# Attention probabilities scaled before they are transposed, values as the stationary operand

## The chip, the cores and the metric

One core of a Trainium2 chip runs the whole program. The engines are TensorE (PE; the loads of its stationary operand are a row of their own, PEld), VectorE (DVE), ScalarE (ACT), GpSimd (POOL) and SyncE (SP), which issues nearly all DMAs. The metric is the device time of one execution in microseconds (us), less is better.

## The reference

Local attention (4 batches, 8 heads, 512 local and 32 global positions, head size 64), then a gated feed-forward block with an RMS norm, then a second feed-forward block with a rational activation.

```python
s_g = scale * q_g @ [k_g, k_l].T;  out_g = sm(s_g) @ [v_g, v_l]
s_ll = where(|i - j| <= 32, scale * q_l @ k_l.T, -1e9)
s_l = [scale * q_l @ k_g.T, s_ll]; out_l = sm(s_l) @ [v_g, v_l]
sm(s) = e / (sum(e) + 1e-9),  e = exp(s - max(s))
x = concat(out_g, out_l) as (4*544 rows, 512 features)
xn = x / rms(x) * rms_g
x = (silu(xn @ w_gate) * (xn @ w_val)) @ w_out
h = x @ w_in;  g = P(h) / (Q(h) + 1e-6);  out = g @ w_out2
```

## The kernel before

**Local attention.** The work is cut into 32 pieces s: a batch, a pair of heads (hp) and a half (u) of the 512 queries. For a piece, 256 queries of two heads are taken in windows of 32 queries, and each window sees 96 local keys and the 32 global ones, so that the scores of a piece are four blocks of 128 queries by 128 keys. Block i = 2c + hf is column half c of head hf; within a block the four windows j stand on partition groups of 32. A piece goes through four stages. `scores(s)` (L353 to L382): 32 short matmuls into two PSUM banks psS, four masked maxima on DVE (L377), four exponentials on ACT (L382) into the tile p. `trans(s)` (L384): four 128x128 transposes on PE into psT (L387), and one ACT copy to pt. `pv(s)` (L391): 16 matmuls into psO (L397), each with a 32-query slice of pt as the stationary operand and 65 columns of vw as the moving one: 64 features and a column of ones, which makes the sum of the row's exponentials. The four windows j use four column strips of the array. DVE then adds 1e-9 (L407), takes the reciprocal (L408) and scales the psO block into on (L410). `out(s)` (L412): two transposes on PE into psX (L416), since the next block wants features on partitions, and an ACT copy into x (L420).

**Global attention** has 8 quads qd of four heads: `g_scores` (psG, L428 and L432; exponentials with their sums at L440 and L441), `g_trans` (five transposes in two banks psGT, L452), `g_pv` (20 matmuls into psOg, L459, and the scaling on DVE, L471), `g_out` (a transpose into psGX, L478, and two DVE copies into x, L482).

**Both share PSUM.** Eight banks are in three rotations: "big" has four (psS, psG and the gate and value products psg, psv of the first feed-forward block), "t" has two (psK, psQ, psKG, psT, psGT, psX, psGX), "o" has two (psO, psOg, and of the feed-forward block psA and psN). A new tile of a rotation waits until the tile two (or four) before it has been read out.

**Order.** The outer loop runs t from 0 to LAST = 32 + TAIL - 1. `step(t)` (L492) makes the transposed keys and queries of piece t (psK, psQ, both from L325), takes piece t-1 through `trans`, t through `scores`, t-2 through `pv` and t-3 through `out`, with the quads of global attention at fixed steps. Between the parts it calls units of the first feed-forward block (60 of its 288 units are issued within the attention; they start at t = 5). A scheduler then orders each engine's instructions; attention has the higher priority (offset 50), the norms (L586 on, three stages for each block of rows, psN at L593) one higher still. The norm of a block is set up at t % 4 == 2. Weights are fetched, split and converted in steps on ACT, DVE and POOL (L83 to L109) from the start on. DMAs of the attention are issued by SP in a fixed order (`dma`, L212 to L219): the load of the values of piece s+4 stands in `pv(s)`, as it overwrites the values that `pv(s)` reads, and everything that SP issues later is behind it.

Of the kernel before, what the change touches and what calls it, by code (L numbers as in the profile page):

```python
# [128 lines left out]
class Attention:  # L129
# [3 lines left out]

    NP = B * H // 2
    NS = 2 * NP
    TAIL = 4
    VW = 65

    def __init__(self, tc, pool, x, stage, q_l, k_l, v_l, q_g, k_g, v_g, more):
        self.tc, self.nc, self.pool, self.x = tc, tc.nc, pool, x  # L140
# [61 lines left out]
        for vw in self.vw[2:]:  # L202
            nc.gpsimd.memset(vw, 1.0)
        nc.gpsimd.memset(self.pg[:, 544:], 0.0)
        self.kts, self.qts, self.pt, self.ptt, self.on, self.gq, self.stage = {}, {}, {}, {}, {}, {}, {}
        for i in range(2):
            self.spread_v(i)
            self.load_v(2 + i)
# [53 lines left out]
            self.dma(out=self.gin[32 * i : 32 * i + 32], in_=g[b].rearrange("h j d -> j h d"))  # L262

    def load_v(self, s):

        b, hp, u = self.place(s)
        t = self.vw[s % 4]  # L270
        v = self.v_l[b, 2 * hp]
        dma = self.dma

        def cut(h0, h1, w0, w1):
            dma(
                out=t[32:64, h0:h1, w0:w1, 0:D],
                in_=bass.AP(
                    tensor=v.tensor,
                    offset=v.offset + (h0 * SL + 32 * (8 * u + w0 - 1)) * D,
                    ap=[[D, 32], [SL * D, h1 - h0], [32 * D, w1 - w0], [1, D]],  # L280
                ),
            )

        for hf in range(2):
            cut(hf, hf + 1, (b, hp, u, hf) == (0, 0, 0, 0), 9 if (b, hp, u, hf) == (B - 1, 3, 1, 1) else 10)
        if u == 1:
            for hf in range(2):
                vg = self.v_g[b, 2 * hp + hf]
                dma(
                    out=t[96:128, hf, 1:9, 0:D],  # L290
                    in_=bass.AP(tensor=vg.tensor, offset=vg.offset, ap=[[D, 32], [0, 8], [1, D]]),
                )
# [60 lines left out]
    def scores(self, s):  # L353
        nc = self.nc
        b, hp, u = self.place(s)
        kt, qt, kg = self.kts[4 * b + hp], self.qts.pop(s), self.kgt[b % 2]
        ps = [self.bank(0, f"psS{s}_{hf}") for hf in range(2)]
        for c in range(2):
            for j in range(4):
                w = 8 * u + 4 * c + j  # L360
                for k0, keys in ((0, kt[:, 32 * w : 32 * w + 96]), (96, kg[:, hp, :])):
                    for hf in range(2):
                        rows = slice(64 * hf, 64 * hf + 64)
                        nc.tensor.matmul(  # L364
                            ps[hf][32 * j : 32 * j + 32, 128 * c + k0 : 128 * c + (96 if k0 == 0 else 128)],
                            qt[rows, 128 * c + 32 * j : 128 * c + 32 * j + 32],
                            keys[rows],
                            start=True, stop=True,
                        )
        p = self.work.tile([128, 4, 128], F32, tag="p", name=f"p{s}", bufs=self.wb[0])  # L370
        self.pt[s] = p
        nm = self.nm[:, s % 4]
        for c in range(2):
            m = self.masks[2 if (u, c) == (1, 1) else (0 if (u, c) == (0, 0) else 1)]
            for hf in range(2):
                i = 2 * c + hf
                self.last_ttr = nc.vector.tensor_tensor_reduce(  # L377
                    out=p[:, i], in0=ps[hf][:, 128 * c : 128 * c + 128], in1=m, scale=-SCALE, scalar=3.0e38,
                    op0=ALU.add, op1=ALU.min, accum_out=nm[:, i : i + 1],
                )  # L380
        for i in range(4):
            self.last_exp = nc.scalar.activation(out=p[:, i], in_=p[:, i], func=AF.Exp, scale=-1.0, bias=nm[:, i : i + 1])  # L382

    def trans(self, s):  # L384
        nc, p, ps = self.nc, self.pt.pop(s), self.bank(1, f"psT{s}")
# [3 lines left out]
        nc.scalar.activation(out=o, in_=ps, func=AF.Copy)  # L389

    def pv(self, s):  # L391
        nc, o, ps, v = self.nc, self.ptt.pop(s), self.bank(2, f"psO{s}"), self.vw[s % 4]
        for c in range(2):
            for hf in range(2):
                i = 2 * c + hf
                for j in range(4):
                    nc.tensor.matmul(  # L397
                        ps[32 * j : 32 * j + 32, self.VW * i : self.VW * i + D + 1],
                        o[:, 128 * i + 32 * j : 128 * i + 32 * j + 32],
                        v[:, hf, 4 * c + j + 1, 0 : D + 1],  # L400
                        start=True, stop=True,
                    )
        if s + 4 < self.NS:
            self.load_v(s + 4)
        ps = ps[:, 0 : 4 * self.VW].rearrange("q (i d) -> q i d", i=4)
        dn = self.dn[:, s % 4]
        nc.vector.tensor_scalar_add(dn, ps[:, :, D], 1e-9)  # L407
        nc.vector.reciprocal(out=dn, in_=dn)  # L408
        self.on[s] = on = self.work.tile([128, 4, D], F32, tag="on", name=f"on{s}", bufs=2)
        nc.vector.tensor_tensor(out=on, in0=ps[:, :, 0:D], in1=_ap(dn, [[1, 4], [0, D]]), op=ALU.mult)  # L410

    def out(self, s):  # L412
        nc, on, ps = self.nc, self.on.pop(s), self.bank(1, f"psX{s}")
        b, hp, u = self.place(s)
        for c in range(2):
            nc.tensor.transpose(  # L416
                ps[:, 128 * c : 128 * c + 128], on[:, 2 * c : 2 * c + 2, :].rearrange("q h d -> q (h d)"), self.ident
            )
        xo = self.x[b][hp // 2][:, hp % 2, SG + 256 * u : SG + 256 * u + 256]
        nc.scalar.activation(out=xo, in_=ps[:, 0:256], func=AF.Copy)  # L420

    def g_scores(self, qd):
# [16 lines left out]
        gs = self.gs[:, qd % 2]  # L439
        nc.scalar.activation(out=P[:, 0:512], in_=ps[0], func=AF.Exp, scale=SCALE, bias=gm[:, 0:1], accum_out=gs[:, 0:1])  # L440
        nc.scalar.activation(out=P[:, 512:544], in_=ps[1][:, 0:SG], func=AF.Exp, scale=SCALE, bias=gm[:, 0:1], accum_out=gs[:, 1:2])  # L441

    def g_trans(self, qd, part):
        nc, P = self.nc, self.pg
# [9 lines left out]

    def g_pv(self, qd):
        nc, o, ps = self.nc, self.gq.pop(qd), self.bank(2, f"psOg{qd}")
        for n in range(5):
            for g in range(4):
                nc.tensor.matmul(  # L459
                    ps[32 * g : 32 * g + 32, 0:D],  # L460
                    o[:, n, 32 * g : 32 * g + 32],
                    self.vn[(2 * qd + g // 2) % 3][:, g % 2, n],
                    start=(n == 0),
                    stop=(n == 4),
                )
        gs = self.gs[:, qd % 2]
        nc.vector.tensor_scalar(out=gs[:, 0:1], in0=gs[:, 0:1], scalar1=gs[:, 1:2], scalar2=1e-9, op0=ALU.add, op1=ALU.add)
        nc.vector.reciprocal(out=gs[:, 0:1], in_=gs[:, 0:1])
        og = self.pool.tile([128, 2, D], F32, tag="og", name=f"og{qd}", bufs=1)
        self.gq[qd] = og  # L470
        nc.vector.tensor_scalar(  # L471
            out=og, in0=_ap(ps, [[0, 2], [1, D]]), scalar1=gs[:, 0:1], scalar2=None, op0=ALU.mult
        )

    def g_out(self, qd):
        b, hq = divmod(qd, 2)
        ps = self.bank(1, f"psGX{qd}")
        self.nc.tensor.transpose(ps[:, 0:128], self.gq.pop(qd).rearrange("q h d -> q (h d)"), self.ident)  # L478
        for hf in range(2):
            rows = slice(64 * hf, 64 * hf + 64)  # L480
            src = ps[rows, 0:128].rearrange("d (p h i) -> d p h i", p=2, h=2)[:, :, hf, :]
            self.nc.vector.tensor_copy(self.x[b][hq][rows, :, 0:SG], src)  # L482

    def advance(self, s, to):

        if not 0 <= s < self.NS:
            return
        while self.stage.get(s, 0) < to:
            now = self.stage[s] = self.stage.get(s, 0) + 1
            (self.scores, self.trans, self.pv, self.out)[now - 1](s)  # L490

    def step(self, t, between):  # L492

# [12 lines left out]
        elif t in (0, 1):  # L506
            self.spread_v(t + 2)
        if t in (4, 8):
            for to in (2, 3, 4):
                for s in range(t - 4, t):  # L510
                    self.advance(s, to)
                    between()
# [6 lines left out]
            self.load_vn(4 * b + i - 3)  # L519
        between()  # L520
        self.advance(t - 2, 3)
        self.advance(t - 3, 4)
        for q0, first in ((0, 4), (1, 5)):
            n = i - first
            if t < NS:
                qd = 2 * b + q0
                if n == 0:
                    self.g_scores(qd)
                if n == 1:
                    between()  # L530
                    self.g_trans(qd, 0)
                    self.g_trans(qd, 1)
                if n == 2:
                    self.g_pv(qd)
                    if q0 == 0:
                        self.load_vn(2 * qd + 3)
                    between()
                    self.g_out(qd)


class FFN1:
# [247 lines left out]
def kernel(  # L789
# [7 lines left out]
    nc = tc.nc  # L797
# [76 lines left out]
    for t in range(LAST + 1):  # L874
# [8 lines left out]
            unit()  # L883
        if t == 2:
            load_consts()
        if t % 4 == 2 and t > 12:
            norms.append(ffn.norm(ORD[(t - 6) // 4]))
        elif t in (4, 8):
            norms.append(ffn.norm(ORD[t // 4 - 1]))
        with tc.high_priority(offset=200):  # L890
# [107 lines left out]
```

## Time and profile before

| | us |
|---|---|
| median of 3 runs | 1048.06 (1048.04 to 1048.88) |
| the profiled execution | 1043.17 |
| its span, first to last instruction | 1041.4 |
| PE busy in the span | 987.8 (95%) |
| DVE busy | 779.1 (75%) |
| ACT busy | 633.0 (61%) |
| POOL busy | 189.2 (18%) |

The mean granted clock of TensorE is 0.977 of full speed. In the page's chain that ended last PE has 80%, DVE 9%, DMA 5%, ACT 3% and SP 1%. Attention lasts from the start to about 300 us. The rest of the span is the two feed-forward blocks, whose instructions the change does not touch.

### The profile page before, as it was taken

Reading aid. Unit: us, or ns where it says so; the run is one execution under the profiler, and the core shown is the slowest. Engines: PE = TensorE matmul, PEld = TensorE weight load, DVE = VectorE, ACT = ScalarE, POOL = GpSimd, SP = SyncE. Lnnn points to the kernel's source line nnn. Section 1 sums busy time; section 2 is a strip of 40 time slices with the busy share of each in tenths; the row PEclk is TensorE's granted clock in tenths of the full one; section 3 lists DMA queues with packets and bytes.
Section 4 is the critical chain, followed back from the end, with each engine's and each line's share of the span. In section 5 each row is a group of like instructions: output and inputs, shape, how many; then the busy total and the mean of one; then the engine's idle time right before and its main releaser. Section 6 shows DMA issues by size and latency. Waiting matters only on the chain.

```text
span 1041.4 us, 23568 instructions
## 1 busy us (share of the span) xinstructions
PE 987.8 (95%) x9376; PEld 900.6 (86%) x9376; DVE 779.1 (75%) x1848; ACT 633.0 (61%) x1442; POOL 189.2 (18%) x220
## 2 busy tenths in 40 slices
PE   7578989999989999999999999999999999999997
PEld 5366877887879999999999999989899889899895
DVE  6586553655549899884896444898988989889897
ACT  4546554645457774553754323777777778777685
POOL 5333221202120000000000002321222222222222
PEclk8669999999999999999999999999999999999999
DMA  9733645353143421542501106200000000000000
GB/s 239 202 106 80 142 115 130 82 142 82 31 165 140 163 82 50 212 166 82 179 24 41 42 1 202 82 1 24 8 1 31 1 2 31 1 32 1 1 31 21
DMA packets 103311, 82.38 MB, mean 79 GB/s; under 512 B 63137, under 2 KB 90785, under 8 KB 103201
## 3 DMA queue, kind: packets, MB, share of 16 engines
q1 hardware_dynamic: 101472, 74.58, 24.2%
q0 software_dynamic: 1728, 6.29, 1.8%
q8 instruction: 74, 1.21, 0.5%
q14 instruction: 37, 0.30, 0.1%
HBM read 62.64 MB, written 10.75 MB: 70 GB/s over the span
## 4 chain that ended last, share of the span: by engine, by line
PE 80%; DVE 9%; DMA 5%; ACT 3%; SPq 1%; issue 1%; POOL 0%; ACTq 0%; POOLq 0%; DVEq 0%
PE psH L731 6%; PE psH L733 6%; PE psH L732 6%; PE psB L767 6%; PE psB L768 6%; PE psB L769 5%; PE psg L625 5%; PE psA L653 4%; PE psv L625 4%; PE psg L626 4%; PE psv L626 4%; PE psA L655 4%; PE psA L654 4%; PE psv L629 4%; PE psg L629 4%; PE psS L364 3%
## 5 line engine op out<-in xcount | busy, mean ns | idle before, releaser
L758 POOL TENSOR_TENSOR gl<-p,gh 128x384 fp32r<-128x384 f32 (+1 forms) x94 | 95.2, 1013 | 281.2 <-ACT gh L756 239.1
L731 PE MATMUL psH<-yt,w_h 128*128 128x384 f32 (+1 forms) x384 | 125.6, 328 | 0.5 <-DVE y L661 0.5
L732 PE MATMUL psH<-yt,w_h 128*128 128x384 f32 (+1 forms) x384 | 125.6, 327 | 0.0
L733 PE MATMUL psH<-yt,w_h 128*128 128x384 f32 (+1 forms) x384 | 123.5, 328 | 0.0
L625 PE MATMUL psg<-xt,w_g 128*128 128x288 f32 (+1 forms) x384 | 113.8, 299 | 7.7 <-ACT xt L615 7.6
L653 PE MATMUL psA<-ah,w_o 128*128 128x288 f32 (+1 forms) x384 | 112.8, 297 | 2.4 <-DVE y L661 1.1
L625 PE MATMUL psv<-xt,w_v 128*128 128x288 f32 (+1 forms) x384 | 111.1, 292 | 0.0
L626 PE MATMUL psv<-xt,w_v 128*128 128x288 f32 (+1 forms) x384 | 110.7, 290 | 0.0
L767 PE MATMUL psB<-w_p,gh 128*128 128x512 f32 x272 | 108.0, 397 | 2.9 <-ACT gh L756 2.9
L626 PE MATMUL psg<-xt,w_g 128*128 128x288 f32 (+1 forms) x384 | 110.3, 290 | 0.0
L654 PE MATMUL psA<-ah,w_o 128*128 128x288 f32 (+1 forms) x384 | 109.9, 290 | 0.0
L655 PE MATMUL psA<-al,w_o 128*128 128x288 f32 (+1 forms) x384 | 109.4, 290 | 0.0
L768 PE MATMUL psB<-w_p,gh 128*128 128x512 f32 x272 | 107.5, 395 | 0.0
L629 PE MATMUL psv<-xt,w_v 128*128 128x288 f32 (+1 forms) x384 | 103.4, 291 | 0.0
L629 PE MATMUL psg<-xt,w_g 128*128 128x288 f32 (+1 forms) x384 | 102.6, 289 | 0.0
L741 DVE SCALAR_TENSOR_TENSOR q<-q,bv,t 128x384 f32<-128x384 f32 (+1 forms) x96 | 67.6, 704 | 29.6 <-ACT q L739 29.4
L769 PE MATMUL psB<-w_p,gl 128*128 128x512 f32 x272 | 84.7, 395 | 0.0
L625 PEld LDWEIGHTS psg<-xt,w_g 128*128 128x128 f32 x384 | 72.7, 190 | 10.5 <-ACT xt L615 8.2
L751 ACT ACTIVATE r<-q,cq 128x384 f32<-128x384 f32 (+1 forms) x96 | 57.6, 600 | 36.7 <-DVE q L741 36.0
L653 PEld LDWEIGHTS psA<-ah,w_o 128*128 128x128 f32 x384 | 72.9, 190 | 4.4 <-DVE y L661 1.5
L731 PEld LDWEIGHTS psH<-yt,w_h 128*128 128x128 f32 x384 | 72.3, 188 | 3.9 <-DVE y L661 0.8
L732 PEld LDWEIGHTS psH<-yt,w_h 128*128 128x128 f32 x384 | 72.3, 188 | 3.7
(176 smaller groups left out, 2635.6 us busy)
## 6 DMA issues: line engine op xcount, KB each, us to landing
raw_h<-in_moe_w_in_dram SPq DMA_DIRECT2D x16, 512.0 KB, 3.7
raw_p<-in_moe_w_out_dram SPq DMA_DIRECT2D x16, 512.0 KB, 4.5
vw<-vw SPq DMA_DIRECT2D x56, 130.0 KB, 2.6
raw_g<-in_moe_w_gate_dram SPq DMA_DIRECT2D x12, 512.0 KB, 4.2
raw_v<-in_moe_w_val_dram SPq DMA_DIRECT2D x12, 512.0 KB, 5.2
raw_o<-in_moe_w_out_dram SPq DMA_DIRECT2D x12, 512.0 KB, 6.0
vw<-in_v_l_dram SPq DMA_DIRECT2D x62, 80.0 KB, 2.5
out_dram<-o SPq DMA_DIRECT2D x17, 256.0 KB, 2.0
```

The source lines that it names most:

```text
L625: nc.tensor.matmul(ps[j], part(j, 0, c), xt[c][:, 0], start=(c == 0), stop=False)
L626: nc.tensor.matmul(ps[j], part(j, 1, c), xt[c][:, 0], start=False, stop=False)
L629: nc.tensor.matmul(ps[j], part(j, 0, c), xt[c][:, 1], start=False, stop=(c == 3))
L653: nc.tensor.matmul(ps, wh, ah, start=(i == 0), stop=False)
L654: nc.tensor.matmul(ps, wl, ah, start=False, stop=False)
L655: nc.tensor.matmul(ps, wh, al, start=False, stop=(i == 3))
L731: nc.tensor.matmul(ph[:, :n], wh, yt[c][:, 0, :n], start=(c == 0), stop=False)
L732: nc.tensor.matmul(ph[:, :n], wl, yt[c][:, 0, :n], start=False, stop=False)
L733: nc.tensor.matmul(ph[:, :n], wh, yt[c][:, 1, :n], start=False, stop=(c == 3))
L767: nc.tensor.matmul(acc[m], gh[:, sl], wh, start=(k == 0), stop=False)
L768: nc.tensor.matmul(acc[m], gh[:, sl], wl, start=False, stop=False)
L769: nc.tensor.matmul(acc[m], gl[:, sl], wh, start=False, stop=(k == NC2 - 1))
```

## The change

Local attention: the exponentials also deliver their sums (`accum_out`). DVE adds 1e-9, takes the reciprocal and multiplies the whole tile p (128x512) by it before it is transposed. In `pv` the operands are exchanged: the 64 columns of a head's values are the stationary operand, a 32-query slice of pt is the moving one, and the two heads use two column strips of 64. The result has features on partitions, and ACT copies it from psO straight into x. The column of ones is no longer read, `out` is gone, and psO is released by ACT instead of DVE. Global attention is changed in the same way: pg (128x544) is scaled on DVE, `g_pv` has the values as the stationary operand, and one DVE copy brings psOg into x; `g_out` is gone. TAIL is 2, and the norm of a block is set up one step earlier.

```diff
@@ class Attention
-    TAIL = 4
-    VW = 65
+    TAIL = 2
+    VW = D
...
@@ scores
+        dn = self.dn[:, s % 4]
         for i in range(4):
-            self.last_exp = nc.scalar.activation(out=p[:, i], in_=p[:, i], func=AF.Exp, scale=-1.0, bias=nm[:, i : i + 1])
+            self.last_exp = nc.scalar.activation(
+                out=p[:, i], in_=p[:, i], func=AF.Exp, scale=-1.0, bias=nm[:, i : i + 1], accum_out=dn[:, i : i + 1]
+            )
+        nc.vector.tensor_scalar_add(dn, dn, 1e-9)
+        nc.vector.reciprocal(out=dn, in_=dn)
+        nc.vector.tensor_tensor(out=p, in0=p, in1=_ap(dn, [[1, 4], [0, 128]]), op=ALU.mult)
 
     def trans(self, s):
         nc, p, ps = self.nc, self.pt.pop(s), self.bank(1, f"psT{s}")
@@ -389,33 +394,21 @@
         nc.scalar.activation(out=o, in_=ps, func=AF.Copy)
 
     def pv(self, s):
+
         nc, o, ps, v = self.nc, self.ptt.pop(s), self.bank(2, f"psO{s}"), self.vw[s % 4]
+        b, hp, u = self.place(s)
         for c in range(2):
-            for hf in range(2):
-                i = 2 * c + hf
-                for j in range(4):
+            for j in range(4):
+                for hf in range(2):
+                    k0 = 128 * (2 * c + hf) + 32 * j
                     nc.tensor.matmul(
-                        ps[32 * j : 32 * j + 32, self.VW * i : self.VW * i + D + 1],
-                        o[:, 128 * i + 32 * j : 128 * i + 32 * j + 32],
-                        v[:, hf, 4 * c + j + 1, 0 : D + 1],
+                        ps[64 * hf : 64 * hf + 64, 128 * c + 32 * j : 128 * c + 32 * j + 32],
+                        v[:, hf, 4 * c + j + 1, :],
+                        o[:, k0 : k0 + 32],
                         start=True, stop=True,
                     )
         if s + 4 < self.NS:
             self.load_v(s + 4)
-        ps = ps[:, 0 : 4 * self.VW].rearrange("q (i d) -> q i d", i=4)
-        dn = self.dn[:, s % 4]
-        nc.vector.tensor_scalar_add(dn, ps[:, :, D], 1e-9)
-        nc.vector.reciprocal(out=dn, in_=dn)
-        self.on[s] = on = self.work.tile([128, 4, D], F32, tag="on", name=f"on{s}", bufs=2)
-        nc.vector.tensor_tensor(out=on, in0=ps[:, :, 0:D], in1=_ap(dn, [[1, 4], [0, D]]), op=ALU.mult)
-
-    def out(self, s):
-        nc, on, ps = self.nc, self.on.pop(s), self.bank(1, f"psX{s}")
-        b, hp, u = self.place(s)
-        for c in range(2):
-            nc.tensor.transpose(
-                ps[:, 128 * c : 128 * c + 128], on[:, 2 * c : 2 * c + 2, :].rearrange("q h d -> q (h d)"), self.ident
-            )
         xo = self.x[b][hp // 2][:, hp % 2, SG + 256 * u : SG + 256 * u + 256]
         nc.scalar.activation(out=xo, in_=ps[:, 0:256], func=AF.Copy)
 
@@ -439,6 +432,9 @@
         gs = self.gs[:, qd % 2]
         nc.scalar.activation(out=P[:, 0:512], in_=ps[0], func=AF.Exp, scale=SCALE, bias=gm[:, 0:1], accum_out=gs[:, 0:1])
         nc.scalar.activation(out=P[:, 512:544], in_=ps[1][:, 0:SG], func=AF.Exp, scale=SCALE, bias=gm[:, 0:1], accum_out=gs[:, 1:2])
+        nc.vector.tensor_scalar(out=gs[:, 0:1], in0=gs[:, 0:1], scalar1=gs[:, 1:2], scalar2=1e-9, op0=ALU.add, op1=ALU.add)
+        nc.vector.reciprocal(out=gs[:, 0:1], in_=gs[:, 0:1])
+        nc.vector.tensor_scalar(out=P[:, 0:544], in0=P[:, 0:544], scalar1=gs[:, 0:1], scalar2=None, op0=ALU.mult)
 
     def g_trans(self, qd, part):
         nc, P = self.nc, self.pg
@@ -454,32 +450,19 @@
 
     def g_pv(self, qd):
         nc, o, ps = self.nc, self.gq.pop(qd), self.bank(2, f"psOg{qd}")
-        for n in range(5):
-            for g in range(4):
-                nc.tensor.matmul(
-                    ps[32 * g : 32 * g + 32, 0:D],
-                    o[:, n, 32 * g : 32 * g + 32],
-                    self.vn[(2 * qd + g // 2) % 3][:, g % 2, n],
-                    start=(n == 0),
-                    stop=(n == 4),
-                )
-        gs = self.gs[:, qd % 2]
-        nc.vector.tensor_scalar(out=gs[:, 0:1], in0=gs[:, 0:1], scalar1=gs[:, 1:2], scalar2=1e-9, op0=ALU.add, op1=ALU.add)
-        nc.vector.reciprocal(out=gs[:, 0:1], in_=gs[:, 0:1])
-        og = self.pool.tile([128, 2, D], F32, tag="og", name=f"og{qd}", bufs=1)
-        self.gq[qd] = og
-        nc.vector.tensor_scalar(
-            out=og, in0=_ap(ps, [[0, 2], [1, D]]), scalar1=gs[:, 0:1], scalar2=None, op0=ALU.mult
-        )
-
-    def g_out(self, qd):
         b, hq = divmod(qd, 2)
-        ps = self.bank(1, f"psGX{qd}")
-        self.nc.tensor.transpose(ps[:, 0:128], self.gq.pop(qd).rearrange("q h d -> q (h d)"), self.ident)
-        for hf in range(2):
-            rows = slice(64 * hf, 64 * hf + 64)
-            src = ps[rows, 0:128].rearrange("d (p h i) -> d p h i", p=2, h=2)[:, :, hf, :]
-            self.nc.vector.tensor_copy(self.x[b][hq][rows, :, 0:SG], src)
+        for p in range(2):
+            for n in range(5):
+                for hf in range(2):
+                    k0 = 64 * p + 32 * hf
+                    nc.tensor.matmul(
+                        ps[64 * hf : 64 * hf + 64, 32 * p : 32 * p + 32],
+                        self.vn[(2 * qd + p) % 3][:, hf, n],
+                        o[:, n, k0 : k0 + 32],
+                        start=(n == 0),
+                        stop=(n == 4),
+                    )
+        nc.vector.tensor_copy(self.x[b][hq][:, :, 0:SG], ps[:, 0:64].rearrange("d (p i) -> d p i", p=2))
 

...
@@ advance, step, and the loop over t
-            (self.scores, self.trans, self.pv, self.out)[now - 1](s)
+            (self.scores, self.trans, self.pv)[now - 1](s)
...
-        self.advance(t - 3, 4)
...
-                    between()
-                    self.g_out(qd)
...
-        if t % 4 == 2 and t > 12:
-            norms.append(ffn.norm(ORD[(t - 6) // 4]))
+        if t % 4 == 1 and t > 12:
+            norms.append(ffn.norm(ORD[(t - 5) // 4]))
```

What stands on PE around one `pv` in the middle of the program, before. A row is a run of equal instructions; 32x65 x16 means 16 matmuls with 32 stationary columns and 65 moving ones, and the number in a tile's name is its piece.

```order
1194 L655 MATMUL psA0_0_3_2927<-al0_3_2366,w_o_3_1442 128x288
1195 L397 MATMUL psO17_2941<-vw1_101,pt17_2714 32x65 x16
1196 L416 MATMUL psX16_2964<-ident_112,on16_2814 128x128
1197 L325 MATMUL psQ20_2968<-ident_112,qin0_89 128x128 x2
1198 L416 MATMUL psX16_2964<-ident_112,on16_2814 128x128
1199 L397 MATMUL psO18_3065<-vw2_102,pt18_2866 32x65 x16
1200 L387 MATMUL psT19_2977<-ident_112,p19_2916 128x128 x4
1201 L364 MATMUL psS20_0_2998<-kt0_92,qt20_2969 32x96
```

The block of 16 passes is whole, and the output transposes psX stand beside the other transposes. The same engine with the change, at a place of the same kind:

```order
1396 L635 MATMUL psA0_3_2_3480<-al3_3_3081,w_o_3_1405 128x256
1397 L404 MATMUL psO21_3494<-pt21_3252,vw1_101 64x32 x8
1398 L324 MATMUL psQ23_3404<-ident_112,qin1_90 128x128 x2
1399 L404 MATMUL psO21_3494<-pt21_3252,vw1_101 64x32 x3
1400 L392 MATMUL psT22_3413<-ident_112,p22_3302 128x128 x4
1401 L404 MATMUL psO21_3494<-pt21_3252,vw1_101 64x32 x5
1402 L458 MATMUL psOg5_3516<-ptg5_3394,vn1_105 64x32 x7
```

No psX is left, and the block of a piece is cut in three by transposes here. In the startup, DVE's order before, from the maxima of the second piece on:

```order
40 L331 COPY kt2_94<-psK2_357 128x512
41 L407 TENSOR_SCALAR dn_109<-psO0_426 128x4
42 L408 RECIPROCAL dn_109<-dn_109 128x4
43 L410 TENSOR_TENSOR on0_447<-psO0_426,dn_109 128x256
44 L377 ISA p2_417,nm_108<-psS2_0_383,mask1_153 128x128
45 L377 ISA nm_108 128x1
```

and with the change, where the scaling of p2 stands between a copy of keys and the conversion of the weights (cv0):

```order
54 L376 ISA nm_108 128x1
55 L330 COPY kt3_95<-psK3_458 128x512
56 L385 TENSOR_SCALAR dn_109<-dn_109 128x4
57 L386 RECIPROCAL dn_109<-dn_109 128x4
58 L387 TENSOR_TENSOR p2_423<-p2_423,dn_109 128x512
59 L91 TENSOR_SCALAR cv0_556<-cv0_556 128x512
60 L92 TENSOR_SCALAR cv0_556<-cv0_556 128x512
```

The division has moved from behind the second product to ahead of the transposes, and its multiplication has 512 columns in place of 256.

## Rows read from the trace of the kernel before

**Rows 1.** Busy us of PE, PEld, DVE, ACT, POOL; PEclk; DMA share; GB/s.

```profile
100.00:200.00 100.00, 93.99 (x1793) 78.84 (x1795) 53.58 (x230) 54.54 (x154) 21.66 (x29) 0.98 0.51 120
200.00:300.00 100.00, 92.93 (x1647) 79.16 (x1643) 52.92 (x213) 50.06 (x140) 21.32 (x30) 1.00 0.32 75
```

**Rows 2.** Waits of PE, 100 to 310 us: total, times, longest us.

```profile
PE psQ L325 <- ACT x L420: 3.7, 7, 0.6
...
PE psGX L478 <- ACT p L382: 1.2, 2, 0.6
...
PE psX L416 <- DVE on L410: 0.7, 1, 0.7
PE psGX L478 <- DVE og L471: 0.6, 1, 0.6
```

**Rows 3.** Timeline of PE around 187 us: start, us, instruction, operands, count.

```profile
187.09 0.30 PE L654 MATMUL psA<-ah,w_o 128*128 128x288 f32 x1
187.22 0.29 PE L655 MATMUL psA<-al,w_o 128*128 128x288 f32 x1
187.44 0.66 PE L397 MATMUL psO<-vw,pt 128*32 128x65 f32 x32
188.04 0.33 PE L416 MATMUL psX<-ident,on 128*128 128x128 f32 x1
```

**Rows 4.** Timeline of PE and PEld around 193 us, 64-column weights.

```profile
192.57 0.14 PEld L428 LDWEIGHTS psG<-kt,qgz 128*64 128x64 f32 x2
192.63 0.14 PEld L428 LDWEIGHTS psG<-kt,qgz 128*64 128x64 f32 x2
...
193.48 0.20 PE L432 MATMUL psG<-kgt,qgz 128*64 128x32 f32 x2
193.51 0.23 PE L432 MATMUL psG<-kgt,qgz 128*64 128x32 f32 x2
```

**Rows 5.** Groups by line on PE, 95 to 300 us: count, busy, mean ns.

```profile
L397 PE MATMUL psO<-vw,pt 128*32 128x65 f32 x800 | 19.7, 223 | 0.4 <-PE psS L364 0.3
...
L416 PE MATMUL psX<-ident,on 128*128 128x128 f32 x54 | 13.4, 293 | 0.9 <-DVE on L410 0.7 <-DVE x L482 0.2
...
L459 PE MATMUL psOg<-vn,ptg 128*32 128x64 f32 x240 | 7.3, 224 | 0.0
```

**Rows 6.** Timeline of PE around 174 us: transposes, one behind a wait.

```profile
173.23 0.60 PE L325 MATMUL psK<-ident,kin 128*128 128x128 f32 x4
173.66 0.27 PE L416 MATMUL psX<-ident,on 128*128 128x128 f32 x1
174.41 0.44 PE L325 MATMUL psQ<-ident,qin 128*128 128x128 f32 x2 [0.47 <-ACT x L420]
```

**Rows 7.** Groups by line on DVE, 0 to 420 us.

```profile
L410 DVE TENSOR_TENSOR on<-psO,dn 128x256 f32<-128x256 f32 x32 | 13.3, 419 | 0.9 <-PE psX L416 0.2
L105 DVE TENSOR_TENSOR w_g<-cv,w_g 128x512 fp32r<-128x512 f32 x8 | 5.5, 687 | 0.2 <-ACT w_g L104 0.2
...
L408 DVE RECIPROCAL dn<-dn 128x4 f32<-128x4 f32 x32 | 5.5, 173 | 0.6
```

**Rows 8.** Timeline of ACT: an exponential's sum being read.

```profile
49.31 0.21 ACT L440 ACTIVATION_READ_ACCUMULATOR pg<-psG,gm 128x1 f32 x1
49.40 0.29 ACT L441 ACTIVATE pg<-psG,gm 128x32 f32<-128x32 f32 x1
```

**Rows 9.** Timeline of DVE and ACT: piece 9, first maximum and the exponentials.

```profile
103.85 0.29 DVE L377 CUSTOM_DVE_ANT_0 p<-psS,mask 128x128 f32<-128x128 f32 x1
...
104.23 1.27 ACT L382 ACTIVATE p<-p,nm 128x128 f32<-128x128 f32 x4
```

**Rows 10.** Timeline of PE: the last norm in the attention.

```profile
300.70 0.85 PE L593 MATMUL psN<-st,ones 128*128 128x288 f32 x1 [1.94 <-POOL st L590]
```

**Rows 11.** Busy us as in rows 1, in the startup.

```profile
40.00:60.00 20.00, 13.40 (x165) 8.12 (x157) 19.00 (x47) 12.90 (x30) 9.73 (x8) 0.59 0.67 195
```

**Rows 12.** Waits of SP's DMA queue, 0 to 110 us.

```profile
SPq L216 <- PE psO L397: 24.6, 5, 12.8
```

More of the change, by code (lines that the diff above doesn't have):

```diff
@@ L204, in __init__ @@
         nc.gpsimd.memset(self.pg[:, 544:], 0.0)
-        self.kts, self.qts, self.pt, self.ptt, self.on, self.gq, self.stage = {}, {}, {}, {}, {}, {}, {}
+        self.kts, self.qts, self.pt, self.ptt, self.gq, self.stage = {}, {}, {}, {}, {}, {}
         for i in range(2):
@@ L508, in step @@
         if t in (4, 8):
-            for to in (2, 3, 4):
+            for to in (2, 3):
                 for s in range(t - 4, t):
```

## The prediction

> **What bounds the kernel now.** I read the page's busy shares first, then busy times by windows of 100 us, then the waits of PE and its timeline around one piece. The windows decide what an edit is worth. From 100 to 300 us, where 25 of the 32 pieces run their `pv`, PE is busy 93.99 and 92.93 of 100 us at granted clocks of 0.98 and 1.00, while DVE and ACT are busy a little over half [rows 1]. The reader is to see that PE's own work there is nearly the time, and that 13.1 us of idleness in 200 is all that freed waits can give back. Before that, between 40 and 60 us, DVE is busy 19.00 of 20 us and PE 13.40 [rows 11]: the startup waits for DVE, which converts weights and serves the attention together. After 300 us nothing changes but where the attention ends.
>
> So the sum is made of what PE has to do between about 95 and 300 us, and of two corners, startup and tail. It goes against the profiled execution, 1043.17 us (span 1041.4), which lies 4.9 under the median of 1048.06; a difference found there is put on the median.
>
> **The second product.** Before, the passes of one piece start at 187.44 and the next operation starts at 188.04 [rows 3]: 0.60 us for 32 records (each of the 16 matmuls leaves two in the trace). The four column strips work side by side, so these are 8 rounds; with some 0.15 for leaving the block, a round has 0.056. The change puts 64 stationary columns in each pass, so that only two strips fit beside each other and the same 32 records become 16 rounds, each with 32 moving columns instead of 65. What a round costs then depends on whether the loading of 64 columns or the moving of 32 sets it. The nearest rows have exactly that shape: two pairs of records with 64 stationary and 32 moving columns, starting at 193.48 and 193.51, the second lasting 0.03 longer, so that they end at 193.68 and 193.74 [rows 4]. The starts are 0.03 apart, the ends 0.06, and two pairs of loads of the same width start 0.06 apart (192.57, 192.63). I read this as the second pair standing in the array until its weights were in, and take 0.057 for a round: 16 x 0.057 + 0.15 = 1.06, or 0.46 more for a piece. The lower end is 16 x 0.028 + 0.15 = 0.60, no change; the upper end, loads and passes one behind the other, is 16 x (0.057 + 0.028) + 0.15 = 1.51, or +0.91.
> There are 800 records, 25 pieces, behind 95 us [rows 5]: 25 x 0.46 = **+11.5** (0 to +23).
>
> The Trainium skill's page "TensorE: Matmul & The Clock Gate", section "Architectural detail: the array is 16× 32×32, not 1× 128×128", says that a matmul can begin while other parts of the array are still loading. By that rule the round would be the short one and this term nothing; the 0.03 by which the second pair lasts longer speaks against it here, the early start of that pair for it.
>
> **Global product.** 240 records for 6 quads, 40 for a quad [rows 5]: 10 rounds before, 20 after, at the same prices 10 x 0.057 = 0.57 more, **+3.4** (0 to +7).
>
> **Output transposes gone.** Four transposes from 173.23 to 173.66 are 0.108 apart [rows 6]. 54 of psX [rows 5] and 6 of psGX go: 60 x 0.108 = **-6.5**.
>
> **More changes of shape.** Between 187.09 and 187.22 the pitch of equal matmuls is 0.13; from 187.22 into the 32-column passes it is 0.22 [rows 3], 0.09 for one change of shape. Counted in the order of PE from the ninth set of keys on, there are 56 more changes of shape with the change, because the blocks of `pv` and `g_pv` are cut up by transposes and scores. 56 x 0.09 would be +5; some stand beside a wait and cost nothing: **+4** (0 to +6).
>
> **Waits that go.** The t rotation of PSUM loses two of its users, psX and psGX, so a tile's predecessor has been read out long before. Waits on it are 3.7, 1.2, 0.7 and 0.6 [rows 2], and five more rows like them, 0.2 to 0.6 each, make 7.8 us in 16 waits. Each also empties the array: behind one, from 173.66 to 174.41 there are 0.75 for an idle time of 0.47 and a pitch of 0.108 [rows 6], so 0.17 more; 16 x 0.17 = 2.7. Of these 10.5 I leave 1.5, since psT8, psK6, psQ10 and psT9, and psQ15, psQ31 and psT30 still stand close behind one another in the new order: **-9** (-10.5 to -4).
>
> **Waits that come.** Between exponentials and transposes DVE now has an addition and a reciprocal (0.173 each at most) and a product of 128x512, 0.687 by the row of that shape [rows 7]; ACT reads four sums, which delay the next instruction by 0.09 each (49.31 to 49.40) [rows 8]. That is about 1.4 us between the last exponential and the first transpose; for piece 9 the chain from the first maximum to the last exponential took 103.85 to 105.50 [rows 9], so it grows from 1.65 to some 3.1. The transposes stand at the head of PE's queue, and all of PE behind them waits too. In the new order PE has 3.2 us or more of other work between the scores and the transposes of most pieces, which covers that; pieces 8, 9 and 17 have 1.5, 1.7 and 2.4, and fall short by 1.6, 1.4 and 0.7. Two quads have psOg too close behind their second psGT (0.4 each), and the last piece has psO31 straight behind psT31 (0.6). Of these 5.1 I take **+4** (+1 to +9), as the ends of chains in a row overlap. On DVE the addition waits for the last exponential, and copies of keys and products of the feed-forward block stand behind it; DVE is busy 54 of 100 us there [rows 1], which covers this and the longer product (0.687 for 0.419 [rows 7]). On ACT the copy to x now waits for the passes themselves, with the next exponentials behind it, and ACT is as idle.
>
> **Tail.** With two steps instead of four, the last psX and its wait go, and the last norm's matmul, which stood 1.94 for POOL [rows 10], may be set up a step earlier: **-1.5** (-3 to 0).
>
> **Startup.** DVE loses four output scalings of 0.419 and gains products of 0.687 for five pieces and one quad before the conversions are done, some 2.4 us in all, in a stretch where it has no idle time [rows 11]. The cover is thin: SP's loads of weights stand behind the load of the next values, which waits for `pv` (24.6 us in 5 waits [rows 12]), and ACT's order has the copy of pt3 some 2.7 us later, behind exponentials of piece 4 and conversions. Since the first units wait for both weights and norm, I take **+1.5** (0 to +5).
>
> **Sum.** 11.5 + 3.4 - 6.5 + 4 - 9 + 4 - 1.5 + 1.5 = 7.4, say +7: 1050 against the profiled execution, 1055 against the median. The likeliest's own range, from the bounds that move together least, is 1050 to 1061.
>
> **Rivals.**
> *The passes are as short as their 32 columns* (chance 0.15). For it: the pair in rows 4 starts 0.03 behind the first. Against: it ends 0.06 behind. The two product terms, 14.9, go: 1055.5 - 14.9 = 1040.6, faster. The point from which the sign turns is a round of 0.043, where half of them is gone. The Trainium skill's rule above would bring this case.
> *The freed waits and the order pay for the passes* (0.22). PE has 13.1 us of idle time in 100 to 300 [rows 1], of which 7.8 are taken above. If the looser order takes another 3 of the rest, and the new waits (4) do not come since units of the feed-forward block stand ahead of the transposes, it is 1055.5 - 7 = 1048. Against: the new order cuts the blocks up, which costs where it helps. Here faster has 0.10, the same 0.10, slower 0.02.
> *The startup slips* (0.14). DVE is full there [rows 11] and SP's queue holds the weights behind `pv` of the first pieces [rows 12]; if that load goes out 2.7 late, and the queue behind it, ACT's and DVE's conversions each add their own delay, 2.7 + 2.4 + a wait of the same size again for the first norm, and it is +9.5 instead of +1.5: 1063. For it: PE is busy 13.40 of 20 us there, so it has nothing to hide a slip with. Against: later units are not tied to the start of the first, and PE has a backlog to work on.
> The forecast itself has 0.49, of which slower 0.42, the same 0.05 and faster 0.02.
>
> **How the numbers follow.** Apart from no change a measurement here can tell 0.2%, 2.1 us. Faster: 0.15 + 0.10 + 0.02 = 0.27. The same: 0.10 + 0.05 = 0.15. Slower: 0.42 + 0.02 + 0.14 = 0.58. The likeliest is 1055. Cases of both signs hold a good share, so the range for 8 in 10 reaches from 1045, below the second rival, to 1066, above the startup's slip; it leaves out the first rival and the far end of serial loads.
>
> **What would show it.** In the new trace the passes of one whole piece should take 1.06 us instead of 0.60, with pairs 0.057 apart; 0.60 or less means the first rival. PE's waits for x in front of psQ should be gone, and waits for p in front of psT stand at pieces 8, 9 and 17. PE's busy time from 100 to 300 us should rise by about 3 us in each 100, and the first psg should start at most 2 us later than before (later by 5 or more: the third rival). The forecast is wrong if the attention's last psT ends earlier than before, or if time is lost at places that have no `pv`.

## The result, and the profile after

| | before | after |
|---|---|---|
| median, us | 1048.47 (4 runs, 1048.04 to 1050.01) | 1064.35 (4 runs, 1061.36 to 1067.24) |
| ratio | | 1.0149, 95% interval 1.0112 to 1.0185 |
| the profiled execution | 1043.17 | 1062.13 |
| its span, granted clock | 1041.4, 0.977 | 1060.4, 0.961 |

The changed kernel is slower by 15.9 us, in the range of 1045 to 1066 and on the side that was forecast, 9 us above the forecast of 1055. The profiled execution of before is a low one: in the experiments' sessions the kernel before took 1042 to 1054 us. So the spans of the two traces lie 19.0 us apart, the medians 15.9.

The windows of 100 us of the changed kernel (columns as in [rows 1]), and the one of the startup [rows 11]:

```profile
100.00:200.00 100.00, 95.47 (x1728) 84.25 (x1729) 59.27 (x227) 56.31 (x201) 23.73 (x30) 0.98 0.41 96
200.00:300.00 100.00, 98.80 (x1653) 87.15 (x1649) 55.13 (x205) 52.36 (x181) 21.04 (x27) 0.97 0.37 88
...
40.00:60.00 20.00, 10.11 (x123) 8.88 (x123) 19.39 (x37) 12.20 (x30) 8.37 (x7) 0.50 0.62 184
```

PE's busy time from 100 to 300 us has risen by 1.48 and 5.87. Its waits there (as [rows 2]) hold no psX, and no x in front of psQ:

```profile
PE psQ L324 <- DVE ptg L449: 2.1, 2, 1.2
PE psN L573 <- POOL st L570: 1.9, 1, 1.9
PE psQ L324 <- DVE kt L330: 0.9, 1, 0.9
PE psT L392 <- DVE p L387: 0.9, 1, 0.9
```

The last norm in the attention (as [rows 10]):

```profile
319.87 1.12 PE L573 MATMUL psN<-st,ones 128*128 128x288 f32 x2 [1.95 <-POOL st L570]
```

One block of `pv` at full clock (as [rows 3]), and the groups by line from 95 to 320 us (as [rows 5]):

```profile
102.15 0.38 PE L324 MATMUL psQ<-ident,qin 128*128 128x128 f32 x2
102.47 1.12 PE L404 MATMUL psO<-pt,vw 128*64 128x32 f32 x32
103.52 0.38 PE L606 MATMUL psv<-xt,w_v 128*128 128x256 f32 x1
...
L404 PE MATMUL psO<-pt,vw 128*64 128x32 f32 x800 | 37.4, 226 | 0.7 <-ACT pt L394 0.7
L458 PE MATMUL psOg<-ptg,vn 128*64 128x32 f32 x242 | 12.0, 231 | 0.0
```

From 102.47 to 103.52 are 1.05 us, where the block before took 0.60. The forecast was 1.06.

**Where the 19 us are.** PE's windows of 5 us: busy us (records), granted clock, DMA share, GB/s:

```profile
75.00:80.00 5.00, 2.65 (x91) 1.00 0.27 63
80.00:85.00 5.00, 4.69 (x60) 0.62 0.02 5
85.00:90.00 5.00, 4.32 (x85) 0.50 0.59 135
90.00:95.00 5.00, 5.00 (x29) 0.50 0.72 203
95.00:100.00 5.00, 5.00 (x38) 0.67 0.43 98
...
290.00:295.00 5.00, 5.00 (x39) 0.50 0.00 0
295.00:300.00 5.00, 5.00 (x50) 0.88 0.00 0
300.00:305.00 5.00, 5.00 (x38) 0.81 0.01 3
305.00:310.00 5.00, 5.00 (x30) 0.50 0.00 0
310.00:315.00 5.00, 5.00 (x38) 0.67 0.00 0
```

TensorE ran at the lower of its two levels (1.2 instead of 2.4 GHz, granted clock 0.50) from 81 to 98 us, around 289 to 296 and from 303 to 313, and for 3.4 us at 108 and 6.9 at 320. Behind 65 us that makes 46.9 us at half clock; before it was 9.9. What PE did before the first of these falls, and before the one at 303:

```profile
78.40 0.86 PE L448 MATMUL psGT<-ident,pg 128*128 128x128 f32 x5 [1.61 <-DVE pg L437]
80.31 0.66 PE L319 MATMUL psQ<-ident,y 128*64 128x128 f32 x8 [1.05 <-DVE ptg L449]
...
298.22 0.24 PE L363 MATMUL psS<-kgt,qt 64*32 64x32 f32 x2
298.40 0.30 PE L404 MATMUL psO<-pt,vw 128*64 128x32 f32 x2
298.63 0.21 PE L363 MATMUL psS<-kgt,qt 64*32 64x32 f32 x1
```

At 78 to 80 it waited for the scaled pg and for the copy behind it, 2.66 us in all. Before, the wait for that copy was there alone, and the clock did not fall:

```profile
80.00 0.66 PE L320 MATMUL psQ<-ident,y 128*64 128x128 f32 x8 [1.14 <-DVE ptg L453]
```

From 298 to 303 it waited for nothing: it alternated, pass by pass, between the scores of piece 31 and the second product of piece 30, which count as busy. It rose again at 98 and at 313 behind a run of matmuls of the feed-forward block. The fall at 289 came behind a wait of 1.20 us for a copy ptg.

For an account I took PE's records from 65 us to the first psN of the last norm in the attention (300.70 before [rows 10], 319.87 after). The time from each start to the next is split: time with no record running is idle; of the rest, the part that the granted clock of that microsecond is below 1 counts as lost to the clock; what remains is full-clock time, by the kind of the two records (second products, transposes, scores, feed-forward block, norm), or "changes" where they are of different kinds. A change so holds the matmul before it too. The kernels e1 to e10 are those of the experiments below.

| us | before | after | e1 | e5 | e8 | e10 |
|---|---|---|---|---|---|---|
| whole stretch | 235.7 | 254.9 | 227.7 | 225.4 | 224.2 | 226.8 |
| idle | 17.6 | 13.1 | 13.4 | 17.9 | 10.9 | 17.9 |
| lost to the clock | 3.0 | 19.5 | 10.7 | 5.2 | 9.3 | 8.0 |
| second products | 18.0 | 33.3 | 31.8 | 16.1 | 32.5 | 15.7 |
| transposes | 34.9 | 24.5 | 23.7 | 34.8 | 23.9 | 35.0 |
| changes (number) | 44.4 (248) | 46.1 (295) | 29.8 (210) | 31.7 (204) | 28.6 (196) | 30.5 (193) |
| all else | 117.7 | 118.5 | 118.2 | 119.8 | 118.9 | 119.5 |

Of 19.2 us more, 16.5 are lost to the clock; PE's work and idle time together make 2.8. The account takes half of each us at half clock as lost, which is an upper figure: matmuls of psA lie 0.12 us apart at full clock and 0.21 at half.

```profile
314.24 0.28 PE L633 MATMUL psA<-ah,w_o 128*128 128x256 f32 x1
314.36 0.28 PE L634 MATMUL psA<-ah,w_o 128*128 128x256 f32 x1
...
322.41 0.41 PE L633 MATMUL psA<-ah,w_o 128*128 128x256 f32 x1
322.62 0.41 PE L634 MATMUL psA<-ah,w_o 128*128 128x256 f32 x1
```

There 0.43 of a us is lost in each; by an estimate from this, 16.5 would be some 14, and 2.8 some 5. The first unit of the feed-forward block starts at 61.6 us (62.3 before), and behind 320 us the distance stays at 19.0.

### The profile page after: what moved, and what is told of

Same layout as the page of the kernel before. It is cut to its first block, busy times and chain, and to the rows that moved or that the text cites. A ratio compares the mean times of both kernels' runs of the same rounds, so it can differ in the third digit from the quotient of the medians.

```text
span 1060.4 us, 23573 instructions
## 1 busy us (share of the span) xinstructions
PE 1009.8 (95%) x9304; PEld 932.4 (88%) x9304; DVE 790.8 (75%) x1840; ACT 642.1 (61%) x1570; POOL 193.1 (18%) x220
## 4 chain that ended last, share of the span: by engine, by line
PE 83%; DVE 9%; ACT 3%; DMA 3%; issue 1%; POOL 1%; POOLq 0%; ACTq 0%; DVEq 0%; SPq 0%
PE psH L711 6%; PE psH L713 6%; PE psH L712 6%; PE psB L747 5%; PE psB L748 5%; PE psB L749 5%; PE psg L605 5%; PE psA L633 4%; PE psv L605 4%; PE psA L634 4%; PE psA L635 4%; PE psg L609 4%; PE psv L606 4%; PE psg L606 4%; PE psv L609 4%; PE psS L363 3%
## 5 line engine op out<-in xcount | busy, mean ns | idle before, releaser
L605 PE MATMUL psg<-xt,w_g 128*128 128x288 f32 (+1 forms) x384 | 115.2, 303 | 2.7 <-ACT xt L595 2.7
L605 PE MATMUL psv<-xt,w_v 128*128 128x288 f32 (+1 forms) x384 | 112.8, 296 | 0.0
L606 PE MATMUL psv<-xt,w_v 128*128 128x288 f32 (+1 forms) x384 | 112.1, 294 | 0.0
L606 PE MATMUL psg<-xt,w_g 128*128 128x288 f32 (+1 forms) x384 | 111.6, 293 | 0.0
L609 PE MATMUL psv<-xt,w_v 128*128 128x288 f32 (+1 forms) x384 | 104.4, 293 | 0.0
L609 PE MATMUL psg<-xt,w_g 128*128 128x288 f32 (+1 forms) x384 | 104.0, 294 | 0.0
```

The source lines that it names most:

```text
L605: nc.tensor.matmul(ps[j], part(j, 0, c), xt[c][:, 0], start=(c == 0), stop=False)
L606: nc.tensor.matmul(ps[j], part(j, 1, c), xt[c][:, 0], start=False, stop=False)
L609: nc.tensor.matmul(ps[j], part(j, 0, c), xt[c][:, 1], start=False, stop=(c == 3))
```

## The experiments

**e1**, blocks kept whole in PE's order:

```diff
 # pv, g_pv
+        with self.tc.high_priority(offset=400):
             ... the matmuls ...
 # scores
+        with self.tc.high_priority(offset=300):
             ... the matmuls ...
```

> The changed kernel with the matmuls of pv and g_pv, and of scores, at a higher priority (400 and 300), so that their blocks stand nearly whole in PE's order: 32 runs of psO instead of 77, 16 of psOg instead of 23, 48 of psS instead of 80, 169 changes of shape instead of 275. Theory C (the time beyond the forecast is TensorE's clock, which falls to half where short passes of two shapes alternate and behind stalls): the fall at 303 us in the run of alternating psS31 and psO30 passes goes, granted clock 0.97 or more, 1050 to 1055. Theory W (the time is PE's own work, as the sum had it, with terms too small): 106 changes of shape x 0.09 = -9.5 at an unchanged clock of 0.96, some 1055. The clock tells them apart, not the time alone.

Measured: 1039.66 us (1039.26 to 1040.49), 0.991 of before (0.988 to 0.9941), 24.7 less than the changed kernel. Granted clock 0.966. The account gives both theories a part: changes -16.3 for 85 fewer, 0.19 each and not 0.09, and the clock -8.8. Theory C's test, 0.97 or more, failed narrowly, and both theories put the time over 10 us too high; the fall at 303 is gone.

**e2, e3**, one half of the change each (the other half as before):

```diff
 # e2: g_scores, g_pv, g_out of the kernel before
 # e3: scores, pv, out, TAIL and the norms of the kernel before
```

> Local attention as changed, global attention as before (scaled behind its product, output transposes psGX). Theory C: the stall of psGT for the scaled pg and of psQ behind it at 77 to 80 us goes, with it the fall of the clock from 81 to 98 us, so that 9 of the 16 us come back: 1053 to 1057. Theory W: psOg's 3.4 us go, 0.6 us of transposes and 2 us of waits come back: 1063 to 1065.

> Global attention as changed, local attention as before. Theory C: the stall for the scaled pg makes the clock fall near 80 us, 1054 to 1059. Theory W: +3.4 for psOg, -0.6 for transposes, -2 for waits: 1048 to 1050.

Measured: 1070.69 (1.0215, 1.0171 to 1.026) and 1061.34 (1.011, 1.0069 to 1.0152). The halves don't add up: +22 and +12 for a whole of +16. e2 missed both expectations: it was at half clock from 80 to 94 us without the scaled pg, behind a wait of 2.69 us for the copy ptg, and at 312 to 319 behind another run of alternating passes. e3 had the fall of theory C, 17.1 us at half clock from 79 on, and was 2 us above its range. But of the 17.5 us between its profiled span and that of before only 6.0 lie ahead of the last norm in the attention; 11.5 lie behind it, 7.4 of them more idle time of PE and 4.0 more lost to the clock, which fell again at 308 and 472. So the price hangs on where the order happens to leave a stall or alternate, and not on one of the halves.

**e4**, the scaling left out:

```diff
-        nc.vector.tensor_scalar_add(dn, dn, 1e-9)
-        nc.vector.reciprocal(out=dn, in_=dn)
-        nc.vector.tensor_tensor(out=p, in0=p, in1=..., op=ALU.mult)
 # and the same three for pg
```

> The changed kernel without the scaling of the probabilities (no addition, reciprocal and product on DVE, local and global), so that the outputs are not divided by their sums; everything else stays. Theory C: the waits for p and pg in front of the transposes are gone, and falls of the clock that followed them: 1050 to 1056, clock 0.97. Theory W: the new waits (4 us) and DVE's startup work (1.5 us) go, the product's 15 us stay: 1058 to 1060, clock 0.96.

Measured: 1076.37 (1.026, 1.0225 to 1.0295), slower than with the scaling. Neither theory held. The half clock stayed (78 to 99 us), without a scaled pg, behind a wait of 2.17 us for the copy ptg. Idle time is as in the changed kernel (12.8 to 13.1), but the order moved again: 362 changes, 59.6 us, against 295 and 46.1. What the scaling's waits cost cannot be read from it.

**e5, e6**, counterparts of e1:

```diff
 # e5: kernel before, pv and g_pv at 400, scores at 300
 # e6: e1, and in the local part
-  matmul(ps[64*hf..., 128*c+32*j...], v[:, hf, 4*c+j+1, :], o[:, k0 : k0+32])
+  matmul(ps[32*j..., 64*i...], o[:, 128*i+32*j ...], v[:, hf, 4*c+j+1, :])
+  DVE copy psO -> on; out(s) with psX, TAIL 4, norms as before
```

> The kernel before with the same priorities as e1 (pv and g_pv 400, scores 300), so that its own blocks stand whole: 33 runs of psO instead of 57, 179 changes of shape instead of 257. Theory O (the gain of e1 is the order's, not the change's): it gains as e1 did, 78 changes x 0.09 to 0.18 = 7 to 14, so 1034 to 1042, level with e1 or better. Theory N (the change is what gains once its blocks are whole): 1045 or more, clearly behind e1's 1039.7.

> e1 with the local second product turned back: probabilities are still scaled ahead of their transposes, but queries are the stationary operand again, a DVE copy takes psO out, output transposes psX return, TAIL and the norms as before; the global part stays changed; same priorities. If the sum's terms hold at equal wholeness: passes -11.5 to -14, transposes +6, waits of psX some +3 to +7, so level with e1 within 4 us, 1036 to 1043. If the wider stationary operand costs through the clock (less of the array moving), it is faster than e1 by 8 or more with a higher clock.

Measured: e5 1035.14 (0.9879, 0.9846 to 0.9912), as theory O had it: the order gives the kernel before 13 us too. Under it the change costs 4.5 by the medians, but the two intervals (to before) overlap and one of e5's four runs took 1041.24, so that this sign is not clear of noise. e6 1048.33 (0.9993, 0.9983 to 1.0004), 5 above its range and 8.7 behind e1, so its second theory (faster than e1 by 8) is out: its clock is higher, 0.973, and full-clock work is about equal (204.6 and 203.5), but idle time is some 24 instead of 13.4. Scaling early and still turning the outputs pays for both.

**e7**, the passes twice:

```diff
+        for _ in range(2):
             ... the matmuls of pv ...
```

> e1 with each local pass of pv issued twice (the second writes the same values), which measures the disputed price by itself. By the sum's 16 rounds x 0.057: 0.91 more for each of 32 pieces; 25 to 27 of them stand where PE sets the time, +23 to +25, some 1063 to 1065, and a whole block takes 1.97 us. By the first rival, 0.028 a round: +11 to 12, some 1051. If the clock matters more than PE's work, it is off by the us at half clock.

Timeline of PE around one whole block of e7:

```profile
134.24 2.06 PE L407 MATMUL psO<-pt,vw 128*64 128x32 f32 x64
136.23 0.40 PE L609 MATMUL psg<-xt,w_g 128*128 128x288 f32 x1
```

1.99 us against 1.97 expected, 0.93 for 16 rounds more. The second products rose from 31.8 to 57.1, +25.3 at full clock, as by 0.057 a round. The time rose by 18.3 only, to 1058.00 (1.0088, 1.0065 to 1.0111), below the 1063 to 1065 by the price alone: e7 lost 3.8 us to the clock where e1 lost 10.7. Short passes in long whole blocks do not by themselves pull the clock down.

**e8, e10**, priorities exchanged (scores 400, pv and g_pv 300), on the changed kernel and on the one before:

```diff
 # pv, g_pv
+        with self.tc.high_priority(offset=300):
 # scores
+        with self.tc.high_priority(offset=400):
```

> e1 with the priorities exchanged (pv and g_pv 300, scores 400): 154 changes of shape instead of 169, 36 runs of psS instead of 48, 37 of psO instead of 32. If changes of shape set the rest: 15 x 0.09 to 0.18, 1 to 3 us less, 1037 to 1039. If the clock does: as its falls come, 1035 to 1050, and the us at half clock say which.

> The kernel before with the priorities of e8 (scores 400, pv and g_pv 300): 172 changes of shape, e8 has 154. If the change itself gains once blocks are whole, this is slower than e8's 1030.4 by over 3 us; if the order alone makes the time, it is 1026 to 1034, as e5 was faster than e1.

Measured: e8 1030.41 (0.9814, 0.9791 to 0.9837), faster than both kernels and below both of its ranges, for the 15 changes fewer and for the clock. e10 1040.75 (0.9925, 0.990 to 0.9949). So here the change gains 10.3, with intervals that lie apart, where under the priorities of e1 it cost 4.5. Of the 8.3 between their profiled spans (1030.4 and 1038.7), the account has 2.6 up to the last norm; 5.7 lie behind it, in a stretch that the change does not touch (741.2 us against 746.9 from that norm to the end). Most of these 5.7 is one wait, which e8 does not have, and the half clock around it (439.8 to 446.6 us): PE is idle 3.0 us more behind the norm in e10 and loses 2.0 more to the clock.

```profile
440.86 0.61 PE L628 MATMUL psg<-xt,w_g 128*128 128x288 f32 x1 [3.28 <-ACT xt L618]
```

In e10 the chain that ended last goes back from there, over ACT, to a load of weights for the second feed-forward block (raw_p, 4.70 us). So more than half of the gain between these two traces lies outside the attention; why the wait comes in e10 and not in e8 is open.

**e9, e11**, fillers in the first stall:

```diff
 # pv, behind the passes, on the changed kernel (e9) and on e8 (e11)
+        if s in (5,):
+            with self.tc.high_priority(offset=500):
+                for _ in range(8):
+                    nc.tensor.matmul(ps[:, 256:512], self.ident, self.kts[3][:, 32:288], ...)
```

> The changed kernel with eight matmuls of 256 columns (ident and keys as operands, into the unused half of psO5) right behind the passes of piece 5, ahead of psGT1. They compute nothing that is used; they fill 1.7 us of the 1.61 us that PE waits there for the scaled pg. Theory C: the clock no longer falls at 81 us, where it stayed at half until 98, so 17 us at half clock, 8 us, come back though PE does more: 1054 to 1059, and the stretch 81 to 98 shows 1.0. Theory W: nothing is gained, 1062 to 1067; the waits behind move by as much as is added.

> e8 with the fillers of e9 behind the passes of piece 5. e8 was at half clock from 78 to 92 us behind two waits (1.81 for pg on ACT, 1.22 for pg on DVE). Theory C: the first wait is filled, the clock does not fall there, 13.6 us at half clock or some 6 us come back: 1024 to 1027. Theory W: 1030 to 1032.

PE's windows and timeline in e9:

```profile
75.00:80.00 5.00, 5.00 (x65) 1.00 0.28 64
80.00:85.00 5.00, 4.12 (x110) 1.00 0.01 3
85.00:90.00 5.00, 3.95 (x74) 1.00 0.65 151
90.00:95.00 5.00, 5.00 (x36) 0.66 0.60 159
95.00:100.00 5.00, 5.00 (x75) 1.00 0.51 126
...
75.95 3.72 PE L413 MATMUL psO<-kt,ident 128*128 128x256 f32 x16
79.51 0.74 PE L452 MATMUL psGT<-ident,pg 128*128 128x128 f32 x5
```

The fall at 81 is gone, which shows that the stall made it; a shorter one at 90 came behind the next wait (1.05 us at 86.88) and passes that alternate with matmuls of the feed-forward block. In e11 the half clock from 78 to 92 is gone altogether. The times did not follow: 1063.02 (1.0136, 1.0095 to 1.0177) and 1030.00 (0.9828, 0.9783 to 0.9873), theory C missed in both, and the times are those of theory W. The fillers took 3.56 us (75.95 to 79.51) to fill 1.61, since each leaves two records, and ate most of the 5.8 us that e9 lost less to the clock (13.7 for 19.5). In e11 the account has 6.2 less lost to the clock, and the stretch to the last norm is as long as in e8 (224.0 and 224.1): 3.3 went to the fillers, the rest into idle time, changes and other work.

**e12**, whole blocks for the last two pieces alone:

```diff
+        with self.tc.high_priority(offset=400) if s >= 30 else nullcontext():   # pv
+        with self.tc.high_priority(offset=300) if s >= 30 else nullcontext():   # scores
```

> The changed kernel with the higher priorities of e1 for pieces 30 and 31 alone, so that psS31 and psO30 no longer alternate pass by pass at the end. In the changed kernel the clock fell at 303 us there, with PE busy all the time, and stayed at half until 314. Theory C: that fall goes, 10 us at half clock or 5 us, and some 3 us of alternating (12 changes there and back): 1054 to 1059. Theory W: only the 3 us, 1060 to 1063, and the fall stays.

PE's windows at the end of the attention in e12:

```profile
295.00:300.00 5.00, 5.00 (x69) 0.57 0.02 3
300.00:305.00 5.00, 5.00 (x41) 1.00 0.00 0
305.00:310.00 5.00, 2.92 (x48) 0.96 0.12 30
310.00:315.00 5.00, 2.59 (x8) 0.50 1.07 366
315.00:320.00 5.00, 5.00 (x26) 0.52 1.09 381
```

Measured: 1057.40 (1.0086, 1.0059 to 1.0113), 7 less than the changed kernel, in theory C's range, but not by its reason. The fall at 303 is gone, which shows that the alternating run made it. Of the 9.2 us that the account gives, 5.6 are changes and 2.3 the clock, since it fell for longer elsewhere, at 108 us and behind the end of the attention; behind 65 us e12 was at half clock for 50.0 us in all, the changed kernel for 46.9.

## Why the prediction was right

Direction and range held; the sum held roughly for PE's work, and a term for the clock was missing from it. That the time fell into the range is in good part luck: PE's work and idle time made less than the +7 of the sum, and the larger part of the 19.0 us came from a cause that no term and no rival named.

- *Second products*: +15.3 in the account, 14.9 forecast; blocks of 1.05 us and e7's price confirm the round of 0.057. The first rival is out. The Trainium skill's page "TensorE: Matmul & The Clock Gate", section "Architectural detail: the array is 16× 32×32, not 1× 128×128", lets a matmul begin while other parts load; if that happens here, it does not bring the round of 64 stationary columns below 0.057.
- *Transposes*: -10.4, forecast -6.5. What refills the array behind their waits, counted in the next term with 2.7, is in it too.
- *Changes of shape*: 47 more in the account, as 56 were counted, but +1.7 for +4. Their price is no constant: e1 took 85 away and gained 16.3, e5 took 44 away and gained 12.7.
- *Waits*: idle time fell by 4.5, where the terms for waits (gone, new, tail) give -9 + 4 - 1.5 = -6.5, of which 2.7 was refill. Piece 17 waited 0.9 for its p, as forecast 0.7; pieces 8 and 9, priced at 1.6 and 1.4, did not wait for theirs, and psQ waited instead, twice, for the copy ptg (2.1). The tail's term failed: the last psN still waits 1.95 for POOL.
- *Startup*: the first unit starts 0.7 earlier, not 1.5 later; the third rival is out.
- *The step that failed* is the first one: "granted clocks of 0.98 and 1.00" were read as given for the changed kernel too. The new waits were priced by their length (1.6 at most), and the cut-up blocks by 0.09 a change; that either would drop the clock, and that PE then works on at half clock, long matmuls too (94 to 98, 292 to 296 us), stood in no term. By the account it cost 14 to 16.5 us between the two traces. Without it the account gives +2.8 to +5, between the second rival's 0 and the forecast's 7.
- *Its own sign of being wrong* came: time was lost at places that have no `pv`, as in these stretches of the feed-forward block at half clock. The other one did not: the last psT ends later than before (316 and 296 us).

What is shown: the stall at 78 us makes the fall at 81 (e9, e11), the alternating run makes the one at 303 (e12). What is not: that the clock alone makes the 15.9, since filling the stall gave no time back, and each experiment moves the whole order. With the order held still, the 35 timed executions of the kernel before in the experiments tend to be longer at a lower clock (correlation -0.6): the two at a granted clock of 0.982 took 1042.46 and 1043.07 us, the three at 0.973 1049.72 to 1053.80. That speaks for a price of the clock, but does not show which of the two makes the other. Why a stall or an alternating run drops it, and how long it then stays low, is open.

## What to carry to other kernels

Exchanging the operands of a small product trades transposes against rounds: here 15.3 against 10.4 us, so it decides little. How a scheduler then cuts the blocks weighed more here: 169 and 154 changes of shape instead of 275, from two priorities, made the changed kernel 24.7 and 33.9 us faster. The same priorities made the kernel before 13 and 8 us faster, so compare both kernels under each order. Price a new wait not by its length alone: look at the granted clock in the windows behind every stall and every run of short alternating passes.

## What was not expected of the hardware

- The granted clock fell at 303 us with PE busy 5.00 of 5 us, when it alternated between two shapes of passes; a PE that the trace shows as busy did not keep its clock there.
- At half clock PE stayed for 17 us (81 to 98), at first with scores, products and transposes, and from 94 on with nothing but 256-column matmuls, behind which the clock rose.
- Alternating costs far more than a change between long blocks: 0.23 us for two records of psO between scores (298.40 to 298.63), where a whole block has 0.066 for two.
